# The first layer of a dense MLP by one level of Strassen's method, with the weights of both layers streamed

## The chip, the core and the metric

The kernel runs on one core of a Trainium2 chip. A core has TensorE (PE, matrix multiplication into PSUM), VectorE (DVE), ScalarE (ACT), GpSimd (POOL) and SyncE (SP, which only issues transfers here); sixteen DMA engines move data between device memory and SBUF. The metric is device time in microseconds for one launch.

## The reference, cut to what matters

Three stages follow one another: a decayed attention (8 batches, 8 heads, 576 tokens, 64 wide), a routed MLP (4608 tokens to 8 experts of 576 tokens each), and a dense MLP, which the change concerns:

```python
def _moe2_ref(x, w_in, w_out):       # x (4608, 512), w_in (512, 2048), w_out (2048, 512)
    h = x @ w_in
    relu6 = np.clip(h + 3.0, 0.0, 6.0)
    g = h * relu6 / 6.0
    return (g @ w_out).astype(np.float32)
```

The weights of the dense MLP are float64. The output is float32.

## The kernel before, in words

Every product is made of three matmuls, because TensorE multiplies a reduced form of float32 (`float32r`): an operand is split into a high half (rounded by ScalarE's copy) and a low half (VectorE: operand minus high half), and high x high, high x low and low x high are added up in PSUM. `mm3` issues the three.

The experts' stage. Expert r has two halves of 288 tokens and eight slices f of 128 hidden columns, 128 units in all. `A` makes a hidden slice (12 matmuls, 288 columns), ScalarE and VectorE split it, `Bm` multiplies it into four accumulators `y0` to `y3` (12 matmuls). `A` runs two units ahead of `Bm`. The experts' weights lie in six slots (`pairs`) of SBUF; the routing of the next experts, their weights' splitting and the gathering of their tokens run beside the matmuls.

The dense stage. The 4608 tokens are cut into NB = 12 blocks of 384, and the 2048 hidden columns into 16 slices f. `C` makes one hidden slice of one block (12 matmuls of 384 columns: 4 slices of the 512 inputs, 3 matmuls each), then ScalarE takes relu(h + 3), VectorE min(., 6) times h, ScalarE the high half, VectorE the low half. `Dm` multiplies it into three accumulators of 128 tokens x 512 (9 matmuls of 512 columns). `C` again runs two units ahead. All weights of both layers are in SBUF when the stage begins and stay there. At the end of a block three tiles `xg` take the accumulators, and GpSimd scatters their rows to the output. `yload` fetches the tokens of the next block (`yT`, what the experts' stage left) and splits them.

`convert` works beside the experts' stage: it turns the float64 weights (32 chunks of 128 x 512) into float32r halves with seven VectorE and three ScalarE instructions a chunk, and stores them in device memory (`w32`), except for the last two groups, which go straight into their slots. `w2load` brings the others into slots that the experts have left.

The order on each engine is fixed when the program is written: the main loop emits matmuls, and after each one `tick` counts down. A side job (`route`, `weights`, `xload`, `convert`, `yload`) is a generator; what it yields is the number of ticks, that is of matmuls, until its next instructions are emitted. So one tick is one matmul of the main loop, and the paces in `PARAMS` (`w_cv` and so on) are counted in them. Each engine then runs its own instructions in that order and waits on semaphores for the others.

Of the kernel before, what the change touches and what calls it, by code (L numbers as in the profile page):

```python
# [89 lines left out]
def _segs(**w):  # L90
    o, d = 0, {}
    for n, x in w.items():
# [8 lines left out]
NB, W2 = 12, 384  # L101
PARAMS = dict(w_first=30, w_cmp=11, w_hop=5, w_hop2=7, w_pe=2, w_low=5, w_pre=22, w_dec=16, w_add=1, w_t=2, w_load=40, w_load0=60, w_gran=16, w_half=8, w_gran0=24, w_gran1=10,
              w_xg=36, w_xg2=50, w_xt=40, w_xt0=4, w_cv=17, w_cv2=6, w_cv3=9, w_w2=60, n_nat=12)
GRAN = ((0, 0), (1, 0), (0, 1), (2, 0), (1, 1), (3, 0), (2, 1), (3, 1))
SLOT = (2, 3, 4, 5, 0, 1, 6, 7)
CONV, DIRECT = (2, 3, 4, 5, 6, 7, 0, 1), 2


class Kern:
# [14 lines left out]
    def later(self, n, do):  # L124
        self.due.append([n, do])
# [5 lines left out]
    def tick(self, n=1):  # L131
        for x in self.due:
            x[0] -= n
        while self.due and self.due[0][0] <= 0:
            self.due.pop(0)[1]()
        for name in list(self.side):
            s = self.side[name]
            s[1] -= n
            if s[1] <= 0:
                self.step(name)  # L140
# [491 lines left out]
    def convert(self):  # L632
# [4 lines left out]
        seq = [(g, w, hf) for g in CONV for w in range(2) for hf in range(2)]  # L637
        direct = 4 * (len(CONV) - DIRECT)

        def issue(i):  # L640
            g, w, hf = seq[i]
# [4 lines left out]
        def pace(late=False):  # L646
            return self.w_cv if "route" in self.side else self.w_cv3 if late else self.w_cv2
# [5 lines left out]
        for i, (g, w, hf) in enumerate(seq):  # L653
            raw, o = raws.pop(0), self.cvo[i % 2]
            if i >= direct:
                while self.pB < (self.w2_old[g] // 4) * 16 + 8 + 2 * (self.w2_old[g] % 4) + 2:
                    yield 1
                o = self.pairs[SLOT[g]][:, w, :, hf * n:hf * n + n]
            lo, hi = raw[:, :, 0], raw[:, :, 1]
            t0 = cv.tile([128, n], I32, name="c_t0")  # L660
# [13 lines left out]
            yield pace(True)  # L674
            V.scalar_tensor_tensor(o[:, 0], ta, 2.0 ** 30 - s0, t0.bitcast(F32), op0=OP.is_le, op1=OP.mult)
            nc.scalar.activation(ta, t1, AF.Copy, scale=2.0 ** -34)
            yield pace(True)
            V.tensor_scalar(t0, o[:, 0].bitcast(I32), -0x800000, None, op0=OP.bitwise_and)
            yield pace(True)
            V.tensor_tensor(o[:, 1], t0.bitcast(F32), ta, OP.mult)  # L680
            if i < direct:
                nc.sync.dma_start(self.w32[g, :, w, :, hf * n:hf * n + n], o.bitcast(F32))
            self.converted = i + 1
            yield pace(True)

    def w2load(self):
        for k, g in enumerate(CONV[:len(CONV) - DIRECT]):
            while self.converted < 4 * k + 4:
                yield 1
            while self.pA < 128 if g > 5 else self.pB < (self.w2_old[g] // 4) * 16 + 8 + 2 * (self.w2_old[g] % 4) + 2:  # L690
                yield 1
            self.nc.gpsimd.dma_start(self.pairs[SLOT[g]], self.w32[g])  # L692
            self.w2_ready = k + 1
            yield self.w_w2

    def need_w2(self, f, w):
        k, direct = CONV.index(f // 2), len(CONV) - DIRECT
        self.run_until("convert", lambda: self.converted >= (4 * k + 2 + 2 * w if k >= direct else 4 * k + 4))
        if k < direct:
            self.run_until("w2load", lambda: self.w2_ready > k)  # L700

    def yload(self):
        nc = self.nc
        for b in range(NB):
            while self.pB < 16 if b == 0 else (self.pD < (b - 1) * 16 or self.pC < b * 16 - (7 if b == 1 else 13)):
                yield 1
            d = self.yacts[b % 2]
            rs = {}

            def issue(k):  # L710
                rs[k] = self.r_p.tile([128, W2], F32, name="yr")
                nc.sync.dma_start(rs[k], self.yT[:, k, b * W2:b * W2 + W2])

            issue(0)
            issue(1)
            yield 40
            for k in range(4):
                x = rs.pop(k)
                nc.scalar.activation(d[0][:, k], x, AF.Copy)
                yield 10  # L720
                nc.vector.tensor_tensor(d[1][:, k], x, d[0][:, k].bitcast(F32), OP.subtract)
                if k + 2 < 4:
                    issue(k + 2)
                yield 20
# [7 lines left out]
    def mlps(self):  # L732
        nc, a = self.nc, self.a
        units = [(1, r, hb, f) for r in range(E) for hb in range(2) for f in range(8)]
        units += [(2, b, 0, f) for b in range(NB) for f in range(16)]
        hts, acc, scat = {}, {}, []
        banks = (("y0", "y1", "y2"), ("y3", "rt", "tp"))

        def A(u):
# [9 lines left out]
            h = self.hg_p.tile([128, 2, 288], FR, name="hg")  # L749
# [6 lines left out]
        def Bm(u):  # L756
# [7 lines left out]
            for d in range(4):  # L764
                c = (f % 2) * 512 + d * 128
                self.mm3(y[d], w[:, 0, c:c + 128], w[:, 1, c:c + 128], h[:, 0], h[:, 1], f == 0, f == 7)
            if f == 7:
                n0 = r * CAP + hb * 288
                last = (r, hb) == (E - 1, 1)
                for d in range(4):  # L770
                    if last and d < 2:
                        o = self.xg_p.tile([128, DM], F32, name="xg")
                    else:
                        o = self.r_p.tile([128, W2], F32, name="r" if d < 2 else "yr")
                    if last and d % 2:
                        nc.vector.tensor_copy(o[:, 0:288], y[d])
                    else:
                        nc.scalar.activation(o[:, 0:288], y[d], AF.Copy)  # L778
# [4 lines left out]
        def C(u):  # L783
            _, b, _, f = u
            self.run_until("yload", lambda: self.y_ready > b)
            if b == 0:
                self.need_w2(f, 0)
            w = self.pairs[SLOT[f // 2]][:, 0]
            y = self.yacts[b % 2]
            p = self.pp.tile([128, W2], F32, name="h", bufs=2)  # L790
            for k in range(NP):
                c = k * 256 + (f % 2) * 128
                self.mm3(p, w[:, 0, c:c + 128], w[:, 1, c:c + 128], y[0][:, k], y[1][:, k], k == 0, k == NP - 1)
            r = self.r_p.tile([128, W2], F32, name="r")
            nc.scalar.activation(r, p, AF.Relu, bias=self.bias[:, 0:1])  # L795
            nc.vector.scalar_tensor_tensor(r, r, 6.0, p, op0=OP.min, op1=OP.mult)  # L796
            g = self.hg_p.tile([128, 2, W2], FR, name="hg")
            nc.scalar.activation(g[:, 0], r, AF.Copy)  # L798
            nc.vector.tensor_tensor(g[:, 1], r, g[:, 0].bitcast(F32), OP.subtract)  # L799
            hts[u] = g  # L800
            self.pC += 1

        def Dm(u):
            _, b, _, f = u
            if b == 0:
                self.need_w2(f, 1)
            w = self.pairs[SLOT[f // 2]][:, 1]
            g = hts.pop(u)
            if f == 0:
                acc[b] = [self.pp.tile([128, 512], F32, name=n) for n in banks[b % 2]]  # L810
            c = (f % 2) * 512
            for t in range(3):
                x = slice(128 * t, 128 * t + 128)
# [153 lines left out]
```

## Time and profile before

| | us |
|---|---|
| median of three runs (lowest, highest) | 1494.48 (1492.3, 1495.27) |
| the profiled execution, its own time | 1491.7 |
| span in its profile, first to last instruction | 1489.3 |

The profiled execution's time is its span and 2.4 us around it; it is 2.8 us below the median of the runs. In rows of the profile, PE is a matmul and PEld the weight load that goes with each; L815 is a line of the kernel before. A matmul's own duration overlaps with the next one's, so the pace is read from the starts.

### The profile page before, as it was taken

The page shows a single profiled execution, that of the slowest core. Times are in us where ns is not written, and L with a number is a line of the kernel's source. Part 1 is how long each engine was busy: PE and PEld are TensorE (multiplying, and loading weights), DVE is VectorE, ACT ScalarE, POOL GpSimd, SP SyncE. Part 2 cuts the span into 40 slices and gives each one's busy share as a digit, 9 for nine tenths or more (in the row PEclk, how much of TensorE's full clock was granted, in tenths as well). Part 3 has the DMA queues.
Part 4 walks back from the last instruction along what each step waited for, and adds up shares of the span by engine and source line. Part 5 has one row for each costly group of instructions (what it writes and reads, how often), then busy time and mean ns, then how long its engine had stood idle before and what let it go on. Part 6 is the DMA issues. An engine that isn't in the chain of part 4 may idle for free.

```text
span 1489.3 us, 27253 instructions
## 1 busy us (share of the span) xinstructions
PE 1423.1 (96%) x11270; PEld 1301.3 (87%) x11270; DVE 702.8 (47%) x1729; ACT 529.9 (36%) x1031; POOL 233.3 (16%) x256
## 2 busy tenths in 40 slices
PE   7899588999999999999999999999999999999998
PEld 5777488989999999999999999999999999999997
DVE  3344557787788798773332323323232323323222
ACT  3233334453444445543332333323232333323222
POOL 6860213122132223000000000000000000000000
PEclk9999799999999999999999999999999999999999
DMA  9991625455464568648010100001010100000000
GB/s 377 378 318 63 234 61 179 160 183 162 134 207 135 176 199 265 190 144 320 22 43 7 37 22 22 32 11 43 1 43 7 37 22 22 32 12 32 1 22 22
DMA packets 60380, 162.90 MB, mean 109 GB/s; under 512 B 7520, under 2 KB 22112, under 8 KB 59488
## 3 DMA queue, kind: packets, MB, share of 16 engines
q1 hardware_dynamic: 41392, 92.10, 18.0%
q0 software_dynamic: 16032, 65.55, 13.3%
q10 hardware_dynamic: 2832, 3.52, 0.7%
q8 instruction: 88, 1.44, 0.4%
q14 instruction: 36, 0.29, 0.1%
HBM read 120.24 MB, written 40.89 MB: 108 GB/s over the span
## 4 chain that ended last, share of the span: by engine, by line
issue 51%; PE 3%; POOL 3%; POOLq 0%; ACT 0%
POOL out_dram L825 2%; PE y L729 2%; PE h L729 2%; POOL nop L831 0%; POOLq L963 0%; POOL big L692 0%; POOLq L825 0%; POOL pair L692 0%; ACT r L778 0%; ACT hg L750 0%; POOLq L692 0%
## 5 line engine op out<-in xcount | busy, mean ns | idle before, releaser
L796 DVE SCALAR_TENSOR_TENSOR r<-r,h 128x384 f32<-128x384 f32 x192 | 106.4, 554 | 445.1 <-ACT r L795 445.1
L729 PE MATMUL h<-big,pair 128*128 128x288 f32 (+1 forms) x1440 | 276.2, 311 | 0.5 <-ACT big L620 0.4
L795 ACT ACTIVATE r<-h,bias 128x384 f32<-128x384 f32 x192 | 111.5, 581 | 439.0 <-PE h L729 439.0
L729 PEld LDWEIGHTS h<-big,pair 128*128 128x128 f32 x1440 | 218.1, 189 | 5.0 <-issue 1.7
L729 PE MATMUL h<-big 128*128 128x288 f32 (+1 forms) x864 | 184.1, 317 | 0.4 <-DVE big L624 0.4
L729 PE MATMUL h<-yact,pair 128*128 128x384 f32 x768 | 173.3, 337 | 0.0
L729 PE MATMUL h<-yact,big 128*128 128x384 f32 x768 | 173.3, 336 | 0.0
L729 PE MATMUL y<-hg,pair 128*128 128x288 f32 x1056 | 167.0, 300 | 1.5 <-ACT r L778 1.5
L799 DVE TENSOR_TENSOR hg<-r,hg 128x384 fp32r<-128x384 f32 x192 | 107.3, 559 | 113.5 <-ACT hg L798 113.5
L825 POOL DMA_INDIRECT out_dram<-xg,idx x36 | 35.1, 975 | 761.4 <-ACT xg L824 754.9
L729 PEld LDWEIGHTS y<-hg,pair 128*128 128x128 f32 x1056 | 146.7, 188 | 3.0 <-ACT r L778 1.7
L815 PE MATMUL y<-pair,hg 128*128 128x512 f32 x576 | 148.9, 394 | 0.0
L815 PE MATMUL y<-big,hg 128*128 128x512 f32 x576 | 148.9, 394 | 0.0
L729 PEld LDWEIGHTS h<-yact,big 128*128 128x128 f32 x768 | 138.5, 188 | 6.4
L729 PEld LDWEIGHTS h<-yact,pair 128*128 128x128 f32 x768 | 138.3, 188 | 6.1
L798 ACT ACTIVATE hg<-r 128x384 fp32r<-128x384 f32 x192 | 100.7, 525 | 119.1 <-DVE r L796 119.1
L729 PEld LDWEIGHTS h<-big 128*128 128x128 f32 x864 | 137.3, 188 | 3.0 <-DVE big L624 0.6
L552 POOL DMA_INDIRECT raw<-in_w_dram,widx x64 | 68.5, 1070 | 361.7 <-issue 66.9
L815 PEld LDWEIGHTS y<-big,hg 128*128 128x128 f32 x576 | 106.7, 188 | 16.8
L815 PEld LDWEIGHTS y<-pair,hg 128*128 128x128 f32 x576 | 106.7, 188 | 16.6
L750 ACT ACTIVATE hg<-h 128x288 fp32r<-128x288 f32 x128 | 52.3, 408 | 120.6 <-PE h L729 112.9
L729 PE MATMUL y<-hg,big 128*128 128x288 f32 x480 | 78.5, 307 | 1.5 <-ACT r L778 1.5
(178 smaller groups left out, 1735.7 us busy)
## 6 DMA issues: line engine op xcount, KB each, us to landing
qk<-in_qk_dram SPq DMA_DIRECT2D x36, 512.0 KB
kv<-in_kv_dram SPq DMA_DIRECT2D x32, 512.0 KB
c_raw<-in_w_dram SPq DMA_DIRECT2D x32, 512.0 KB
w<-big SPq DMA_DIRECT2D x24, 512.0 KB
yr<-yT SPq DMA_DIRECT2D x48, 192.0 KB
big<-w POOLq DMA_DIRECT2D x4, 2048.0 KB
yT<-yr SPq DMA_DIRECT2D x32, 144.0 KB
yT<-r SPq DMA_DIRECT2D x30, 144.0 KB
```

Source lines behind the costliest of these rows:

```text
L552: nc.gpsimd.indirect_dma_start(out=raw, out_offset=None, in_=a[("w1", "w2")[w]], in_offset=bass.IndirectOffsetOnAxis(ap=self.widx[:, r, g: ...
L729: self.nc.tensor.matmul(out, w, x, start=(first and i == 0), stop=(last and i == 2))
L750: nc.scalar.activation(h[:, 0], p, AF.Relu)
L795: nc.scalar.activation(r, p, AF.Relu, bias=self.bias[:, 0:1])
L796: nc.vector.scalar_tensor_tensor(r, r, 6.0, p, op0=OP.min, op1=OP.mult)
L798: nc.scalar.activation(g[:, 0], r, AF.Copy)
L799: nc.vector.tensor_tensor(g[:, 1], r, g[:, 0].bitcast(F32), OP.subtract)
L815: nc.tensor.matmul(acc[b][t], g[:, gw, x], w[:, ww, c:c + 512], start=(f == 0 and i == 0), stop=(f == 15 and i == 2))
L825: ins = nc.gpsimd.indirect_dma_start(out=a["out"], out_offset=bass.IndirectOffsetOnAxis(ap=self.idx[:, 3 * b + t:3 * b + t + 1], axis=0), ...
```

## The change

The first layer of the dense stage takes blocks of 768 tokens (NB = 6) and two hidden slices at once, NS = 8 pairs of slices a block. In one such step, a span here (48 in all), its operands are 2 x 2 blocks: two halves of the 512 inputs, two halves of the 768 tokens, two hidden slices. Instead of eight products of blocks it makes seven of sums of blocks (Winograd's form): each is 6 matmuls of 384 columns. The sums of weights (`s1` to `s4`) are made in `convert`, those of tokens (`t1` to `t4`) in `yload`. The products are summed up partly in PSUM, by going on in a bank that has been read meanwhile, and partly on VectorE, through the tiles `m1`, `u2` and `tv`; `post` does what ScalarE and VectorE did in `C`. The second layer's 36 matmuls a span (`outs`) are those of the span before, and are issued between the products.

The converted weights no longer stay in SBUF. Those of the first layer (seven operands, 14 KB in each partition, 1835 KB a span) and of the second (8 KB, 1049 KB a span) are kept in device memory, `wC` and `wD`, and are fetched again for each span into two slots each, `cw` and `dw`, by `wload` and `dload` on GpSimd's queue.

```diff
-NB, W2 = 12, 384
+W2 = 384
+NB, NS = 6, 8
...
-              w_xg=36, w_xg2=50, w_xt=40, w_xt0=4, w_cv=17, w_cv2=6, w_cv3=9, w_w2=60, n_nat=12)
+              w_xg=36, w_xg2=50, w_xt=40, w_xt0=4, w_cv=14, w_cv2=9, w_cv3=7, w_y=10, w_y0=8, n_nat=12)
 GRAN = ((0, 0), (1, 0), (0, 1), (2, 0), (1, 1), (3, 0), (2, 1), (3, 1))
-SLOT = (2, 3, 4, 5, 0, 1, 6, 7)
-CONV, DIRECT = (2, 3, 4, 5, 6, 7, 0, 1), 2
+OPW, OPY = ("11", "s2", "12", "s3", "s1", "22", "s4"), ("11", "t2", "21", "t3", "t1", "t4", "22")
...
+        def store(o, q, op):
+            x = OPW.index(op) * 512
+            nc.sync.dma_start(self.wC[2 * q:2 * q + 2, :, x:x + 512].rearrange("f p x -> p f x"), two(o).bitcast(F32))
+
+        def split(x, q, op):
+            o = out()
+            h, l = two(o)[:, :, 0:256], two(o)[:, :, 256:512]
+            nc.scalar.activation(h, two(x), AF.Copy)
+            yield pace()
+            V.tensor_tensor(l, two(x), h.bitcast(F32), OP.subtract)
+            yield pace()
+            store(o, q, op)
...
+            if op == "22":
+                V.tensor_tensor(R2, R1, R2, OP.add)
+                yield pace()
+                yield from split(R2, q, "s1")
+            elif op == "11":
+                V.tensor_tensor(R1, x, R1, OP.subtract)
+                yield pace()
+                yield from split(R1, q, "s3")
+                V.tensor_tensor(R2, R2, x, OP.subtract)
+                yield pace()
+                yield from split(R2, q, "s2")
+            elif op == "12":
+                V.tensor_tensor(R2, x, R2, OP.subtract)
+                yield pace()
+                yield from split(R2, q, "s4")
+                self.dC = q + 1
...
+    def wload(self):
+        nc = self.nc
+        for s in range(NB * NS):
+            i = s % NS
+            while s == 0 and not self.freed(28) or s == 1 and not self.freed(29) or s > 1 and self.span < s - 1:
...
+            nc.gpsimd.dma_start(self.cw[s % 2], self.wC[i])
+            self.c_ready = s + 1
...
+    def dload(self):
+        for s in range(NB * NS):
+            i = s % NS
+            while not self.freed(30) or s > 1 and self.span < s:
...
+            self.nc.gpsimd.dma_start(self.dw[s % 2], self.wD[i])
+            self.d_ready = s + 1
...
+                yield from split(b11, "11")
+                t1 = b11
+                V.tensor_tensor(t1, b12, b11, OP.subtract)
+                yield w
+                V.tensor_tensor(b12, b22, b12, OP.subtract)
+                yield from split(t1, "t1")
+                V.tensor_tensor(t1, b22, t1, OP.subtract)
+                yield from split(b12, "t3")
+                yield from split(t1, "t2")
+                yield from split(b21, "21")
+                V.tensor_tensor(b21, b21, t1, OP.subtract)
+                yield from split(b22, "22")
+                yield from split(b21, "t4")
...
+            def prod(p, first):
+                o = n[0]
+                for kt in range(2):
+                    for j, (wh, yh) in enumerate(((0, 0), (0, 1), (1, 0))):
+                        nc.tensor.matmul(p, cw[:, o, wh, kt], y[o][:, yh, kt], start=(first and kt + j == 0),
+                                         stop=(kt == 1 and j == 2), skip_group_check=True)
+                        self.tick()
+                n[0] += 1
...
+            def post(x, key):
+                while open_r[0] > 1:
+                    self.due.pop(0)[1]()
+                open_r[0] += 1
+                r = self.r_p.tile([128, W2], F32, name="r")
+                nc.scalar.activation(r, x, AF.Relu, bias=self.bias[:, 0:1])
+
+                def two():
+                    V.scalar_tensor_tensor(r, r, 6.0, x, op0=OP.min, op1=OP.mult)
+
+                def three():
+                    gs[key] = g = self.gbuf[self.n_g % 5].rearrange("p (a b) -> p a b", a=2)
+                    self.n_g += 1
+                    nc.scalar.activation(g[:, 0], r, AF.Copy)
+
+                    def four():
+                        V.tensor_tensor(g[:, 1], r, g[:, 0].bitcast(F32), OP.subtract)
+                        low.add(key)
+                        open_r[0] -= 1
+
+                    self.later(4, four)
+
+                self.later(4, two)
+                self.later(8, three)
...
+            bank = lambda: self.pp.tile([128, W2], F32, name="h", bufs=2)
+            p = bank()
+            prod(p, True)
+            m1 = self.r_p.tile([128, W2], F32, name="yr")
+            nc.scalar.activation(m1, p, AF.Copy)
+            yield
+            p2 = bank()
+            prod(p2, True)
+            u2 = self.r_p.tile([128, W2], F32, name="yr")
+            V.tensor_tensor(u2, m1, p2, OP.add)
+            yield
+            prod(p, False)
+            post(p, (s, 0, 0))
+            yield
+            prod(p2, False)
+            V.tensor_tensor(tv, m1, p2, OP.add)
+            yield
+            p = bank()
+            prod(p, True)
+            V.tensor_tensor(tv, tv, p, OP.add)
+            post(tv, (s, 1, 1))
+            yield
+            prod(p2, False)
+            V.tensor_tensor(m1, m1, p2, OP.add)
+            post(m1, (s, 1, 0))
+            yield
+            prod(p, False)
+            V.tensor_tensor(u2, u2, p, OP.add)
+            post(u2, (s, 0, 1))
...
+            seq = [(0, t) for t in range(3)] + [(1, t) for t in range(3, 6)] + [(1, t) for t in range(3)] + [(0, t) for t in range(3, 6)]
...
+                for k, (gw, ww) in enumerate(((0, 0), (0, 1), (1, 0))):
+                    if k == 2:
+                        while (s, j, t // 3) not in low:
+                            self.due.pop(0)[1]()
+                    nc.tensor.matmul(acc[b][t], g[:, gw, x], w[:, 512 * ww:512 * ww + 512],
+                                     start=(i == 0 and seen[t] == 0 and k == 0), stop=(i == NS - 1 and seen[t] == 1 and k == 2))
+                    self.tick()
...
+        merge(prods(0), both(), (0, 1, 1) * 4)
+        for s in range(1, NB * NS):
+            merge(prods(s), outs(s - 1), (0, 1, 1) * 5 + (0, 1) * 2)
```

On TensorE in the middle of the dense stage of the kernel before, a group of 12 matmuls of the first layer (`h`, a new bank each time) alternates with 9 of the second (`y0` to `y2` are the accumulators, `yact`, `pair` and `big` hold tokens and weights):

```order
L729 MATMUL h_11487<-yact0_2221,big_2679 128x384 x12
L815 MATMUL y0_11378<-big_2679,hg_11442 128x512 x3
L815 MATMUL y1_11379<-big_2679,hg_11442 128x512 x3
L815 MATMUL y2_11380<-big_2679,hg_11442 128x512 x3
L729 MATMUL h_11517<-yact0_2221,big_2679 128x384 x12
```

In the changed kernel the beginning of a span stands there; `h_10558` and `h_10579` are its two banks, `ring`, `big` and `hgt` hold tokens, weights and hidden tiles:

```order
L876 MATMUL h_10558<-big_2679 128x384 x6
L970 MATMUL y0_10445<-ring_2221 128x512 x3
L970 MATMUL y1_10446<-ring_2221 128x512 x3
L876 MATMUL h_10579<-big_2679 128x384 x6
L970 MATMUL y2_10447<-ring_2221 128x512 x3
L970 MATMUL y3_10448<-ring_2221,hgt_2218 128x512 x3
L876 MATMUL h_10558<-big_2679 128x384 x6
L970 MATMUL rt_10449<-ring_2221,hgt_2218 128x512 x3
L970 MATMUL tp_10450<-ring_2221,hgt_2218 128x512 x3
L876 MATMUL h_10579<-big_2679 128x384 x6
L970 MATMUL y0_10445<-ring_2221,hgt_2218 128x512 x3
L970 MATMUL y1_10446<-ring_2221,hgt_2218 128x512 x3
```

The products came down to groups of 6, two of which (the third and fourth) go on in the banks of the first two, and one or two groups of the second layer, 3 matmuls each, stand between them; after these rows come the products 5 to 7 and five more groups of 3.

On VectorE in the dense stage of the kernel before, the work of three units and the splitting of a next block's tokens (`yact`):

```order
L721 TENSOR_TENSOR yact0_2221<-yr_9947,yact0_2221 128x384
L796 SCALAR_TENSOR_TENSOR r_10034<-r_10034,h_10018 128x384
L799 TENSOR_TENSOR hg_10037<-r_10034,hg_10037 128x384
L721 TENSOR_TENSOR yact0_2221<-yr_9992,yact0_2221 128x384
L796 SCALAR_TENSOR_TENSOR r_10064<-r_10064,h_10050 128x384
L799 TENSOR_TENSOR hg_10067<-r_10064,hg_10067 128x384
```

In the changed kernel these rows stand in the third span: `L915`, `L921` and `L925` are sums of products, `L889` and `L897` belong to `post`, `L788` splits tokens of the second block, and `L705`, `L714`, `L728` and `L672` are the converter's:

```order
L915 TENSOR_TENSOR yr<-yr,h 128x384
L788 TENSOR_TENSOR big<-yq,big 128x384
L705 TENSOR_TENSOR big<-c_t_9475,c_ta 128x2x256
L714 TENSOR_TENSOR c_ta<-big 128x512
L889 SCALAR_TENSOR_TENSOR r<-r,h 128x384
L728 TENSOR_TENSOR rec_2220<-c_ta,rec_2220 128x512
L897 TENSOR_TENSOR hgt<-r,hgt 128x384
L921 TENSOR_TENSOR L<-yr,h 128x384
L788 TENSOR_TENSOR big<-yq,big 128x384
L672 TENSOR_TENSOR big<-rec_2220,big 128x2x256
L925 TENSOR_TENSOR L<-L,h 128x384
L889 SCALAR_TENSOR_TENSOR r<-r,L 128x384
```

The converter and the splitting of tokens, which stood beside the experts' matmuls before, now reach into the first spans and stand between the sums and the hidden tiles.

On GpSimd's queue at the end of the experts' stage of the kernel before, the last converted weights come in and the scatters of the first block follow:

```order
L692 DMA big<-w_77 128x4096 x2
L692 DMA pair_2217<-w_77 128x4096
L692 DMA pair_2218<-w_77 128x4096
L692 DMA big<-w_77 128x4096 x2
L825 DMA out_dram<-xg,idx 4608x512
L831 MEMSET nop 128x1
```

In the changed kernel the first block's weights stand there (`wC` the first layer's, `wD` the second's):

```order
L747 DMA big<-wC 128x3584 x2
L757 DMA ring<-wD 128x2048 x2
L747 DMA big<-wC 128x3584 x2
L757 DMA ring<-wD 128x2048
L747 DMA big<-wC 128x3584
L757 DMA ring<-wD 128x2048
L747 DMA big<-wC 128x3584
L757 DMA ring<-wD 128x2048
L944 DMA out_dram<-xg,idx 4608x512
L950 MEMSET nop 128x1
```

The loads no longer end with the experts: a pair of them stands there for each span, and a block's six scatters stand between two pairs.

## Rows read from the trace of the kernel before

**Rows 1.** The page, parts 1 and 2: busy time, then 40 slices in tenths.
```profile
PE 1423.1 (96%) x11270; PEld 1301.3 (87%) x11270; DVE 702.8 (47%) x1729; ACT 529.9 (36%) x1031; POOL 233.3 (16%) x256
...
DVE  3344557787788798773332323323232323323222
...
DMA  9991625455464568648010100001010100000000
```

**Rows 2.** Windows: the experts, their end, the dense layer (columns: first row).
```profile
core 0: us, PE busy (x) PEld busy (x) DVE busy (x) ACT busy (x) POOL busy (x), PEclk, DMA share, GB/s
240.00:640.00 400.00, 382.09 (x3308) 368.28 (x3308) 316.14 (x905) 187.29 (x373) 93.01 (x88) 0.99 0.57 181
...
683.00:1482.00 799.00, 799.00 (x4006) 723.41 (x4004) 241.21 (x440) 240.33 (x450) 37.90 (x70) 1.00 0.09 31
```

**Rows 3.** Waits of TensorE from 240 to 640 us: total, times, longest.
```profile
engine line waited for: us in total, times, longest us
PE tp L614 <- DMA xg<-xn,idx: 3.9, 3, 2.2
PE y L729 <- ACT r L778: 2.9, 2, 1.5
PE rt L398 <- ACT gs L393: 2.7, 2, 1.5
```

**Rows 4.** Timeline of TensorE in the dense layer: start, length, count.
```profile
1000.56 2.27 PE L729 MATMUL h<-yact,big 128*128 128x384 f32 x12
1002.67 2.24 PE L815 MATMUL y<-big,hg 128*128 128x512 f32 x9
1004.75 2.27 PE L729 MATMUL h<-yact,big 128*128 128x384 f32 x12
```

**Rows 5.** The page, part 5: groups on VectorE and ScalarE, 384 wide.
```profile
L796 DVE SCALAR_TENSOR_TENSOR r<-r,h 128x384 f32<-128x384 f32 x192 | 106.4, 554 | 445.1 <-ACT r L795 445.1
...
L795 ACT ACTIVATE r<-h,bias 128x384 f32<-128x384 f32 x192 | 111.5, 581 | 439.0 <-PE h L729 439.0
...
L799 DVE TENSOR_TENSOR hg<-r,hg 128x384 fp32r<-128x384 f32 x192 | 107.3, 559 | 113.5 <-ACT hg L798 113.5
...
L798 ACT ACTIVATE hg<-r 128x384 fp32r<-128x384 f32 x192 | 100.7, 525 | 119.1 <-DVE r L796 119.1
```

**Rows 6.** Groups by line: the converter, and the low half of an expert's hidden tile.
```profile
L751 DVE SCALAR_TENSOR_TENSOR hg<-h,hg 128x288 fp32r<-128x288 f32 x128 | 58.1, 454 | 35.9 <-ACT hg L750 34.3 <-issue 0.8
...
L665 DVE SCALAR_TENSOR_TENSOR c_t<-c_raw,c_t 128x512 int32<-128x512 int32 x32 | 22.1, 690 | 0.4
...
L680 DVE TENSOR_TENSOR big<-c_t,c_ta 128x512 fp32r<-128x512 f32 x24 | 16.4, 685 | 0.6 <-ACT c_ta L676 0.6
...
L661 DVE TENSOR_SCALAR c_t<-c_raw 128x512 int32<-128x512 int32 x32 | 13.6, 426 | 0.2
```

**Rows 7.** Timeline of weight loads in an expert's layers, twelve to a row.
```profile
642.77 1.65 PEld L729 LDWEIGHTS h<-big,pair 128*128 128x128 f32 x12
644.37 1.65 PEld L729 LDWEIGHTS y<-hg,pair 128*128 128x128 f32 x12
```

**Rows 8.** Timeline of GpSimd: two weight loads of 2048 KB.
```profile
662.57 0.57 POOL L692 DMA_DIRECT2D big<-w  x1 [39.38 <-PE y L729]
668.96 0.55 POOL L692 DMA_DIRECT2D big<-w  x1 [5.83 <-PE y L729]
```

**Rows 9.** Window while those loads run; columns as in Rows 2.
```profile
669.00:676.00 7.00, 7.00 (x53) 7.00 (x52) 4.58 (x9) 2.72 (x5) 0.93 (x2) 1.00 1.01 415
```

**Rows 10.** Timeline of GpSimd: scatters of one block, and the last of the run.
```profile
750.04 1.03 POOL L825 DMA_INDIRECT out_dram<-xg,idx  x1 [65.41 <-ACT xg L824]
751.06 0.12 POOL L831 MEMSET nop<- 128x1 f32 x1
751.37 1.00 POOL L825 DMA_INDIRECT out_dram<-xg,idx  x1 [0.19 <-issue]
...
1484.19 0.97 POOL L825 DMA_INDIRECT out_dram<-xg,idx  x1 [0.19 <-issue]
```

More of the change, by code (lines that the diff above doesn't have):

```diff
@@ L124, in later @@
     def later(self, n, do):
-        self.due.append([n, do])
+        i = len(self.due)
+        while i and self.due[i - 1][0] > n:
+            i -= 1
+        self.due.insert(i, [n, do])
     def flush(self):
@@ L136, in tick @@
         for name in list(self.side):
+            if name not in self.side:
+                continue
             s = self.side[name]
@@ L644, in issue, with pace, out @@
             return raw
-        def pace(late=False):
-            return self.w_cv if "route" in self.side else self.w_cv3 if late else self.w_cv2
+        def pace():
+            return self.w_cv if "route" in self.side else self.w_cv2 if self.span < 0 else self.w_cv3
+        def out():
+            self.n_o += 1
+            return self.cvo[self.n_o % 2]
+        def store(o, q, op):
[9 more added lines that the diff above has]
+            store(o, q, op)
         while self.routed < 2:
@@ L704, in yload @@
         for b in range(NB):
-            while self.pB < 16 if b == 0 else (self.pD < (b - 1) * 16 or self.pC < b * 16 - (7 if b == 1 else 13)):
+            while b and self.span < max(1, NS * (b - 1)):
                 yield 1
[L707 to L715, printed above, removed]
@@ L716, in yload, with piece @@
-            yield 40
[L717 to L724, printed above, removed]
+            op = self.yops[b % 2]
+            w = self.w_y if b else self.w_y0
+            def piece(k, pool):
+                x = yq.tile([128, 2 * W2], F32, name="yq") if pool else self.raw_p.tile([128, 1024], F32, name="raw")[:, 0:2 * W2]
+                nc.sync.dma_start(x, self.yT[:, k, 2 * b * W2:2 * b * W2 + 2 * W2])
+                return x[:, 0:W2], x[:, W2:2 * W2]
@@ new lines, in evict @@
+        def evict(b, t):
+            o = self.xg_p.tile([128, DM], F32, name="xg")
+            if t % 2:
+                V.tensor_scalar(o, acc[b][t], 1.0 / 6.0, None, op0=OP.mult)
+            else:
+                nc.scalar.activation(o, acc[b][t], AF.Copy, scale=1.0 / 6.0)
+            ins = nc.gpsimd.indirect_dma_start(
+                out=a["out"], out_offset=bass.IndirectOffsetOnAxis(ap=self.idx[:, 6 * b + t:6 * b + t + 1], axis=0),
+                in_=o, in_offset=None)
+            for x in scat:
+                self.tc.declare_no_dep(ins.ins, x.ins, reason="each row of out is scattered to once")
+            scat.append(ins)
+            nc.gpsimd.memset(self.nop, 0.0)
@@ new lines, in merge, with both @@
+        def merge(x, y, pat):
+            for c in pat:
+                next((x, y)[c], None)
+            for _ in x:
+                pass
+            for _ in y:
+                pass
+        A(units[0])
+        A(units[1])
+        for i, u in enumerate(units[:-2]):
+            A(units[i + 2])
+            for _ in Bm(u):
+                pass
+        def both():
+            yield from Bm(units[-2])
+            yield from Bm(units[-1])
+        merge(prods(0), both(), (0, 1, 1) * 4)
```

241 lines of the change are left out of this document (120 added, 121 removed).

## The prediction, made before the changed kernel had run

> **What bounds the kernel now.** I read the page first. Matmuls cover 96% of the span [rows 1], and behind the attention the slices show two regimes: from slice 7 to 18 of 40 VectorE is at seven to nine tenths and the DMA engines at about half, and from there VectorE falls to two or three tenths and the DMA engines to nearly nothing. The windows say how tightly TensorE is bound in each. In the dense stage (683 to 1482 us) it is busy for all of 799.00 us [rows 2], so nothing but its own matmuls sets the pace there. In the 400 us of the experts before, it is idle for 17.9 us, with VectorE busy for 316 us of them [rows 2]; the waits are small and many, for routing, gathered tokens and emptied accumulators [rows 3]. So fewer matmuls in the dense stage shorten the run one to one, as long as the other engines and the transfers still fit beside them; and that stage has room: VectorE 30%, DMA 9% [rows 2].
>
> **What is removed.** Pace is read from starts. Twelve matmuls of 384 columns take 1000.56 to 1002.67, 2.11 us or 0.1758 us each; nine of 512 take 1002.67 to 1004.75, 2.08 us or 0.2311 us each [rows 4]. The work of a span was 48 + 36 matmuls, 4 x 4.19 = 16.76 us. It becomes 42 + 36: 7.38 + 8.32 = 15.70 us. Over 48 spans, 288 matmuls of 384 columns go: 288 x 0.1758 = **50.6 us**. The forms stay the same, and the last of 12 matmuls passes to the first of 9 without a gap [rows 4], so the many more changes between the two kinds are priced at nothing. The Trainium skill (TensorE: Matmul & The Clock Gate, Back-to-back issue gap) gives a warm matmul N / 2.4 ns + 2.5 ns; by it 384 columns would be an estimated 162.5 ns, and the gain 46.8 us. The row is 13 ns longer, and I keep the row.
>
> **VectorE in a normal span.** It gets 13 instructions of 384 columns: two for each of four hidden tiles (0.554 and 0.559 us [rows 5]) and five sums. A sum with one operand in PSUM does not occur before; its nearest row is the first of rows 5, which reads PSUM too, so 0.556. That is 7.2 us of 15.70. Each block's tokens add 22 such instructions, 12.2 us over about four and a half spans. ScalarE gets nine (0.525 to 0.581 us [rows 5]), 5 us. Both fit. I also followed the waits of TensorE inside a span, from the order: with a product P at 1.05 us and a group of the second layer O at 0.69, the third product goes on in the first bank 3.8 us after it was filled, and the copy in between takes 0.55. The tightest place is the sum after the sixth product: its bank is wanted by the next span's first product after O, P and O, 2.43 us, and the sum takes 0.56. So VectorE may lag by 1.9 us before TensorE notices. Cost: nothing, and this 1.9 us is the cover.
>
> **VectorE in the first spans.** Here the cover goes. The order puts the last converter instruction into the sixth span, and the second block's tokens are split from the second span on. From the second span's beginning to the converter's end there are 345 ticks: 4.4 spans, 69.4 us of TensorE. VectorE's rows in that stretch are 83 instructions of 384 columns (0.556 us), 30 of 512 (0.688, between the two rows of 0.685 and 0.690) and 16 of the short kind (0.426 [rows 6]): 46.1 + 20.6 + 6.8 = 73.5 us. It is over 100%: 4.1 us too much over the whole, and over its densest 263 ticks I count 6.9 us. Besides, where a hidden tile's second step stands right behind the sum it comes from (the last two rows of the order's VectorE piece), a late VectorE waits for ScalarE's relu of 0.58 us [rows 5] in between; two or three times a span that is up to 6.6 us more. Subtracting the 1.9 us of cover, the loss lies between 2 us (whole stretch, no such waits) and 16 (densest stretch, all the waits, and a lag of 2 to 3 us brought in from the stage before, where I count 37.8 us of VectorE in the 40.0 us of the last 300 expert matmuls at 1.60 us for twelve [rows 6, 7]). With half of the waits it is 5.5 by the whole stretch and 8.3 by the densest; I take **7 us**.
>
> **The converter beside the experts.** Its pace goes from 17 ticks to 14, and sums of weights are added. Between the same two ticks of the routing (303 and 2128) the order has 682 VectorE instructions in place of 671: 23 more of 512 columns at 0.685, and 12 fewer of the others (four each at 0.690, 0.426 and 0.556), 15.8 - 6.7 = 9.1 us more [rows 5, 6]. Its bounds are 0 (all of it falls into gaps) and 9 (all of it delays TensorE). In each of the seven routing rounds about 100 ticks already hold some 7 us more VectorE work than TensorE time, 49 us in all, and TensorE's idle time there is 17.9 [rows 2]; by that ratio, 0.36, it costs **3 us**. The larger number of stores on SP's queue (44 of 512 KB for 24) delays only the storing of expert results, whose buffers have the 25.6 us of the next eight units to come free.
>
> **The streams.** A span needs 1835 + 1049 KB. While loads of 2048 KB followed one another on the same queue, the engines moved 415 GB/s [rows 8, 9]; at that the pair takes 6.9 us. What one transfer costs beyond its bytes no row isolates; the last scatter, 256 KB, was issued at 1484.19 [rows 10] and the span ended at 1489.3, so 5.1 us less its 0.6 is an upper bound, 4.5. Both are issued when a span begins and wanted when the next begins: 11.4 of 15.70 us, so hidden. The first has no span ahead of it: its place in the order is 72 expert matmuls, 9.6 us [rows 7], ahead of the first product; 1835 KB take 4.4 + at most 4.5. Cost 0, at most 3 with the other transfers that run there.
>
> **Blocks' ends.** Six evictions share three `xg` tiles, so the fourth waits for the first's scatter. That begins about 9.9 us into the span, and one scatter is issued every 1.3 us [rows 10]; with the 5.1 us from above VectorE is held to 15.0, evicts, and makes the sixth product's sum by 16.3, where the bank is wanted at 15.7. That is 0 to 0.6 us at each of five block ends: **1 us** (0 to 3). GpSimd's next load stands behind these scatters, some 1 to 2 us late against 4.3 of slack. The end of the run keeps its form, three scatters after the last matmul.
>
> **The sum**, against the profiled execution's 1491.7: 1491.7 - 50.6 + 7 + 3 + 1 = **1452 us**. That execution lies 2.8 us below the median of the runs, which belongs to the range.
>
> **Rivals.** *All covered* (8%): VectorE's lag never passes the cover, and 1491.7 - 50.6 = 1441. For it speaks that routing rounds with 7 us too much cost only 2.6 each; against it, that here the excess is carried on over four spans. *VectorE binds hard* (10%): every upper bound at once, 1491.7 - 50.6 + 16 + 9 + 3 = 1469; it would show as VectorE at nine tenths and more over six spans. *The streams come late* (5%): the case on the other side. It needs loads that are slower beside this stage than [rows 9] shows. With the 11 us above spent, the gain of 1.055 us a span is used up when a span lasts 16.6 us; less 4.5, that is 2884 KB in 12.1 us, 238 GB/s. At 200 GB/s a span lasts 18.9 us and the run 1452 + 47 x 3.2 = 1602. The Trainium skill (SBUF — State Buffer, SBUF: two separate sides) has a mechanism for it: GpSimd, which writes the descriptors of its own queue's transfers, is shut out of a shared port while VectorE runs in a two-port mode. As a mechanism of this kernel: the converter's short instructions (0.426 us for 512 columns, [rows 6]) would be the ones, and two loads issued in the midst of them took 0.57 and 0.55 us on GpSimd [rows 8], so I see no such hold, and after the sixth span those instructions are gone.
>
> **Numbers.** The forecast has 77%. Its range by its own terms is 1443 to 1468 (losses between 2 and 27), which leaves out most of each rival. About 0.2%, 3 us, is what a measurement of this kernel can tell from no change; faster than that is 94%, the same 1%, slower 5%.
>
> **What would show it.** Right: 2016 first-layer matmuls at the same 0.176 us; a dense stage whose spans, from the seventh on, take 15.7 us with no idle TensorE; waits of TensorE for VectorE, some 7 us, in the second to sixth span alone; the experts' stage 3 us longer. Wrong: idle time before first products that DMA ends (the streams), spans above 15.8 us late in the run, or a wait for sums in every span, which would mean that the bank cover of 1.9 us is not what I read.

## The result, and the profile after

The changed kernel took 1453.95 us (median of 4 runs, 1450.24 to 1454.95) against 1494.13 for the kernel before: 0.9728 of its time, 95% interval 0.9708 to 0.9748. The prediction was 1452. The profiled execution took 1453.67 us, its span 1451.9; its page, parts 1, 2, 5 and 6, answers to [rows 1, 5]:

```profile
PE 1378.9 (95%) x10982; PEld 1254.1 (86%) x10982; DVE 892.2 (61%) x2105; ACT 572.2 (39%) x1127; POOL 281.3 (19%) x346
...
DVE  3334556777887888787795564465456446545443
...
PEclk9999789999999999999999999999999999999999
DMA  9992533454644556767867555565555545545551
...
L876 PE MATMUL h<-ring,big 128*128 128x384 f32 x1296 | 262.3, 337 | 2.9 <-DVE yr L929 2.7
...
L876 PE MATMUL h<-big 128*128 128x384 f32 x720 | 145.0, 336 | 0.0
...
big<-wC POOLq DMA_DIRECT2D x48, 1792.0 KB, 7.6
ring<-wD POOLq DMA_DIRECT2D x48, 1024.0 KB, 9.8
...
wC<-big SPq DMA_DIRECT2D x28, 512.0 KB, 3.0
```

The 2016 first-layer matmuls are there, with one wait to speak of before them. The DMA engines, nearly idle in the dense stage before, are now half busy to the end. Windows of the same run, with columns as in [rows 2], show a stretch of one span's length in which the converter still runs, and a long one behind it:

```profile
730.03:745.73 15.70, 15.70 (x79) 13.87 (x78) 15.00 (x31) 9.37 (x18) 0.99 (x3) 1.00 0.80 285
...
840.00:1400.00 560.00, 560.00 (x2786) 503.20 (x2785) 294.23 (x556) 200.57 (x384) 65.88 (x120) 1.00 0.56 206
```

In the second row TensorE has no idle time at all. Even in the first, with VectorE busy for 15.00 of 15.70 us, TensorE does not stop.

To place the rest I cut every run into three by its timeline of TensorE: up to the first expert product, from there to the first dense product, from there to the span's end. Taking 50.6 us from the dense stage before (814.4) leaves 763.8; the last column is what each run spent above that (for the eighth product, above 814.4).

| run | first expert product at | experts' stage | dense stage | above |
|---|---|---|---|---|
| before | 183.8 | 491.1 | 814.4 | |
| before, again | 189.2 | 494.8 | 814.5 | |
| after | 190.6 | 492.3 | 769.0 | 5.2 |
| after, again | 185.7 | 495.0 | 767.8 | 4.0 |
| converter held | 184.6 | 493.2 | 766.4 | 2.6 |
| converter held, again | 185.7 | 493.7 | 765.8 | 2.0 |
| second load later | 184.5 | 494.9 | 772.0 | 8.2 |
| last quarter not stored | 185.6 | 495.2 | 764.1 | 0.3 |
| converter faster beside experts | 184.7 | 505.7 | 766.9 | 3.1 |
| eighth product | 186.4 | 494.5 | 815.4 | 1.0 |
| first-layer loads doubled | 187.8 | 492.5 | 880.3 | 116.5 |

So the first profile lost 5.2 us in the dense stage, most of it at the first span's end: beside the run without the last quarter's stores its third span starts 4.2 us late (682.93 to 714.13 us, for 680.80 to 707.81 there), its sixth 5.0 us (the 0.8 us between are spread in pieces of TensorE's idle time too short to be listed as waits). Pieces of its timelines (SyncE's issues, VectorE, TensorE):

```profile
681.31 0.38 SPq L665 DMA_DIRECT2D wC<-big  x1
...
694.77 0.69 DVE L700 SCALAR_TENSOR_TENSOR big<-c_ta,c_t 128x512 fp32r<-128x512 f32 x1 [2.51 <-DMA wC<-big]
...
696.45 1.40 PE L876 MATMUL h<-ring,big 128*128 128x384 f32 x6 [2.71 <-DVE yr L929]
```

what the view of that one store (L665, 681 to 683 us) says of it:

```profile
who waited for it (us, times):
  DVE big L700: 2.5, 1
...
DMA to landing us min/median/max: 13.4/13.4/13.4
```

and windows of the same time:

```profile
690.00:695.00 5.00, 3.74 (x23) 3.42 (x21) 2.46 (x6) 1.66 (x4) 0.53 (x1) 1.00 1.07 378
695.00:700.00 5.00, 3.55 (x12) 3.07 (x13) 3.51 (x8) 2.49 (x6) 0.00 (x0) 0.76 1.02 373
700.00:705.00 5.00, 5.00 (x24) 4.47 (x24) 4.24 (x9) 2.10 (x5) 0.00 (x0) 0.90 0.99 348
...
698.00:699.00 1.00, 1.00 (x4) 0.73 (x3) 0.97 (x3) 0.05 (x1) 0.00 (x0) 0.50 1.02 416
...
701.00:702.00 1.00, 1.00 (x7) 0.95 (x6) 1.00 (x3) 0.00 (x0) 0.00 (x0) 1.00 0.95 374
```

The converter has two output tiles and fills them in turn. Its next chunk wants the tile whose last contents are still on their way to DRAM: the store issued at 681.31 lands 13.4 us later and lets VectorE go on at 694.77, where the median store took 3.0 us. (The store after it, issued at 687.32 from the other tile, took 8.7 us, and nobody waited for it.) The DMA engines are full, for the first loads of both layers run then. Behind the waiting instruction stands, in order, the sum that empties a bank (L929), and TensorE waits 2.71 us for it. Then its granted clock falls: the 0.76 and 0.90 of the two windows of 5 us are mixtures of the two levels, and windows of 1 us have it at 0.50 (1.2 GHz) from 698 to 701 us and at 1.00 again behind it. By these shares that cost an estimated 1.7 us more. VectorE is busy for only 2.46 of the 5 us from 690: it is held, not overloaded.

**Theory A**: the loss in the first spans is a converter store that lands late on full DMA engines. **Theory B**, the prediction's: it is VectorE's work.

### The profile page after: what moved, and what is told of

It reads as the page before. It is cut to its first block, busy times and chain, and to the rows that moved or that the text cites. A ratio compares the mean times of both kernels' runs of the same rounds, so it can differ in the third digit from the quotient of the medians.

```text
span 1451.9 us, 27422 instructions
## 1 busy us (share of the span) xinstructions
PE 1378.9 (95%) x10982; PEld 1254.1 (86%) x10982; DVE 892.2 (61%) x2105; ACT 572.2 (39%) x1127; POOL 281.3 (19%) x346
## 4 chain that ended last, share of the span: by engine, by line
PE 78%; DVE 11%; DMA 5%; issue 3%; ACT 2%; POOL 0%; POOLq 0%; ACTq 0%; DVEq 0%
PE h L876 22%; PE y L970 17%; PE h L808 10%; PE y L808 9%; PE rt L970 4%; PE tp L970 4%; DMA raw<-in_w_dram,widx 2%; PE ov L248 2%; PE sc L215 2%; DMA wC<-big 1%; DVE ring L576 1%; PE st L245 1%; PE y L327 1%; PE tp L619 1%; PE ov L238 1%
## 5 line engine op out<-in xcount | busy, mean ns | idle before, releaser
L876 PE MATMUL h<-ring,big 128*128 128x384 f32 x1296 | 262.3, 337 | 2.9 <-DVE yr L929 2.7
L876 PEld LDWEIGHTS h<-ring,big 128*128 128x128 f32 x1296 | 232.3, 188 | 23.6 <-DVE yr L929 4.0
L970 PE MATMUL y<-ring,hgt 128*128 128x512 f32 x684 | 180.2, 394 | 0.0
L808 PE MATMUL h<-big,ring 128*128 128x288 f32 x1056 | 171.6, 304 | 1.3 <-DVE hgt L829 0.8
L808 PE MATMUL y<-hgt,ring 128*128 128x288 f32 x1056 | 167.0, 300 | 0.0
L808 PEld LDWEIGHTS h<-big,ring 128*128 128x128 f32 x1056 | 149.4, 191 | 3.9 <-issue 1.7
L808 PEld LDWEIGHTS y<-hgt,ring 128*128 128x128 f32 x1056 | 146.9, 188 | 2.4 <-issue 2.4
L876 PE MATMUL h<-big 128*128 128x384 f32 x720 | 145.0, 336 | 0.0
L970 PEld LDWEIGHTS y<-ring,hgt 128*128 128x128 f32 x684 | 126.7, 188 | 19.9
L897 DVE TENSOR_TENSOR hgt<-r,hgt 128x384 fp32r<-128x384 f32 x114 | 63.5, 557 | 41.6 <-ACT hgt L894 40.4
L889 DVE SCALAR_TENSOR_TENSOR r<-r,h 128x384 f32<-128x384 f32 x48 | 26.6, 554 | 94.4 <-ACT r L886 94.3
L886 ACT ACTIVATE r<-h,bias 128x384 f32<-128x384 f32 x48 | 27.9, 580 | 125.6 <-PE h L876 125.6
```

Source lines behind the costliest of these rows:

```text
L808: self.nc.tensor.matmul(out, w, x, start=(first and i == 0), stop=(last and i == 2))
L876: nc.tensor.matmul(p, cw[:, o, wh, kt], y[o][:, yh, kt], start=(first and kt + j == 0), stop=(kt == 1 and j == 2), skip_group_check=True)
L886: nc.scalar.activation(r, x, AF.Relu, bias=self.bias[:, 0:1])
L897: V.tensor_tensor(g[:, 1], r, g[:, 0].bitcast(F32), OP.subtract)
L970: nc.tensor.matmul(acc[b][t], g[:, gw, x], w[:, 512 * ww:512 * ww + 512], start=(i == 0 and seen[t] == 0 and k == 0), stop=(i == NS - 1 an ...
```

## The experiments

**Both kernels again.** The first profile after also starts its experts 6.8 us later than the one before.

> The changed kernel once more, for a second profile of it. In its first profile the first expert product starts 6.8 us later than in the profile of the kernel before (190.6 against 183.8), with a granted clock of 0.57 and 0.75 in 150 to 170, in a stretch whose instructions are the same in both kernels. If that is a difference between executions, the new profile has the product within some 3 us of 183.8, or at another time than 190.6; if it belongs to the kernel, at 190.6 again. The 5 us lost at the end of the first span of the dense stage (VectorE held 2.5 us by the store of a converted chunk, TensorE waiting 2.7 us, then a granted clock of 0.5) should come back by theory A and by theory B alike. Time by all: 1451 to 1455.

> The kernel before once more, for a second profile of it: whether its first expert product starts at 183.8 again and its granted clock in 150 to 170 is 1.00 again. If the 6.8 us ahead of the experts are a difference between executions, these move by some us here too; if they belong to the changed kernel, they stay within 1 us.

The changed kernel took 1450.23 us in the second series: 0.9723 of before (0.9702 to 0.9745). The kernel before was run once more for its profile, 1500.2 us. Windows of the two new profiles, before first, then after:

```profile
150.00:160.00 10.00, 8.84 (x71) 8.30 (x70) 3.10 (x9) 4.79 (x9) 0.00 (x0) 0.52 0.48 183
160.00:170.00 10.00, 7.67 (x105) 6.74 (x102) 4.99 (x18) 5.34 (x11) 0.00 (x0) 0.97 0.69 264
```

```profile
150.00:160.00 10.00, 7.93 (x99) 7.01 (x98) 4.28 (x15) 5.93 (x12) 0.00 (x0) 0.91 0.65 240
160.00:170.00 10.00, 6.66 (x94) 5.99 (x94) 4.99 (x21) 4.95 (x10) 0.00 (x0) 1.00 0.81 298
```

Now the kernel before is the one at half clock (0.52), with its first expert product at 189.2, and the changed one is at 185.7. Over nine profiles of the kernels with the change in the table that point lies between 184.5 and 190.6: it differs between executions, and the 6.8 us are no effect of the change. In the new profile of after the dense loss is 4.0 us, in waits of 1.04, 0.81 and 1.02 us spread over two spans, the granted clock staying at 1.00; VectorE and ScalarE again wait for `wC<-big` ahead of the first two (0.84 and 3.38 us).

**The converter held back in the first span.**

```diff
+            while self.pB >= 124 and self.span < 1:
+                yield 1
             raw, o = raws.pop(0), out()
```

> The converter begins no chunk during the first span of the dense stage; its work there moves into the spans behind it. Theory A: the 5 us are lost because the converter's store lands late while the first loads of the dense stage fill the DMA engines, so that VectorE, in order, waits 2.5 us for a converter tile and TensorE for VectorE; without chunks there nothing waits, and the time falls by about 4.5 us (2.7 us of wait and 1.8 us at half clock) to 1449. Theory B, the prediction's: VectorE has too much work in the first spans; then more of it in spans 1 to 5 costs as much there, and the time stays at 1454 or rises by up to 3 us.

1447.2 us, 0.9693 (0.9676 to 0.9711), beside 1450.23 on the same chip; their runs do not overlap (1445.93 to 1448.24, 1449.53 to 1454.62). A second series gave 1448.85, 0.9690 (0.9669 to 0.9712). B's "same or slower" falls. (Of the 4.3 us between the two profiled executions only 1.4 lie in the dense stage; the rest lies ahead of it, in the first two columns of the table, where executions differ anyway.) A's 4.5 us were too many: of 4.0, 2.0 to 2.6 stay, for the wait came back, smaller, in the third span (L702 and L931 are L700 and L929 of the changed kernel; VectorE's timeline, then TensorE's):

```profile
717.28 0.69 DVE L702 SCALAR_TENSOR_TENSOR big<-c_ta,c_t 128x512 fp32r<-128x512 f32 x1 [1.86 <-DMA wC<-big]
...
721.74 1.31 PE L878 MATMUL h<-ring,big 128*128 128x384 f32 x6 [1.24 <-DVE yr L931]
```

**The second load of second-layer weights a span later.**

```diff
-            while not self.freed(30) or s > 1 and self.span < s:
+            while not self.freed(30) or s > 0 and self.span < s:
```

> The second load of second-layer weights (1 MB) is issued one span later, so that the stretch in which the DMA engines are full carries 1 MB less; VectorE's work is untouched. Theory A: at the 385 GB/s of that stretch 1 MB takes 2.7 us, the store of the converted chunk lands that much sooner, the wait of 2.7 us goes or shrinks and the half clock behind it with it: 2 to 4.5 us faster, 1449.5 to 1452. Theory B (too much VectorE work): no change.

1453.23 us, 0.9731 (0.9713 to 0.9750): neither theory's number, and some 3 us more than after on the same chip, though the runs of the two overlap (1451.84 to 1454.34, 1449.53 to 1454.62). The dense stage of its profile lost 8.2 us, for 4.0. The timelines of SyncE, ScalarE and TensorE show why:

```profile
695.41 13.41 SPq L665 DMA_DIRECT2D wC<-big  x3
...
707.08 0.63 ACT L670 ACTIVATE big<-rec 128x512 fp32r<-128x512 f32 x1 [6.26 <-DMA wC<-big]
...
708.95 1.32 PE L876 MATMUL h<-ring,big 128*128 128x384 f32 x6 [3.66 <-DVE L L925]
```

and the windows:

```profile
700.00:705.00 5.00, 5.00 (x26) 4.34 (x24) 1.93 (x4) 0.81 (x2) 0.00 (x0) 1.00 1.05 386
705.00:710.00 5.00, 1.34 (x8) 1.05 (x7) 1.52 (x3) 1.64 (x3) 0.00 (x0) 1.00 0.33 126
710.00:715.00 5.00, 4.45 (x14) 3.45 (x13) 4.83 (x11) 3.21 (x7) 1.08 (x2) 0.53 0.80 264
```

The megabyte left one full stretch for another (share 1.05 at 700 to 705), in which the converter has three stores to make. ScalarE waits 6.26 us for the tile of the store issued at 695.41, VectorE for ScalarE, TensorE for VectorE, and the clock halves behind it. My expectation looked at the store that had been late, not at the next ones. The mechanism is A's.

**All arithmetic, the last quarter's stores left out.**

```diff
             x = OPW.index(op) * 512
+            if q == 3:
+                return
...
-            nc.gpsimd.dma_start(self.cw[s % 2], self.wC[i])
+            nc.gpsimd.dma_start(self.cw[s % 2], self.wC[i if i < 6 else i - 2])
```

(the same for `wD`.)

> The converter does all of its arithmetic, but does not store the operands of the last quarter of the weights; spans 6 and 7 of each block load those of spans 4 and 5 instead (part of the output is computed with the wrong weights, with as much work). Theory A, as it stands after the three kernels before: what costs some 4 us in the first three spans is a converter store that lands late on full DMA engines, with ScalarE or VectorE waiting for its tile; without these stores that wait is gone and the time falls to that of the kernel that holds its converter back or below, 1445 to 1447.5. Theory B: it is VectorE's own work there (14.5 to 15 of 15.7 us in spans 2 to 4); that is unchanged, and so is the time, 1450.

1446.39 us, 0.9671 (0.9648 to 0.9694). All waits of TensorE from 683 to 1440 us:

```profile
PE h L879 <- DVE yr L932: 0.3, 1, 0.3
```

and two windows with the converter at work:

```profile
712.20:727.90 15.70, 15.70 (x79) 14.10 (x78) 14.50 (x30) 8.92 (x18) 1.06 (x2) 1.00 0.59 219
...
743.60:759.30 15.70, 15.70 (x79) 14.10 (x78) 15.18 (x32) 9.88 (x20) 1.07 (x2) 1.00 0.42 148
```

VectorE does the same work, 14.50 and 15.18 us of 15.70, and TensorE never waits there: 0.3 us of loss is left of 4 to 5, and the interval of the ratio lies clear of that of after (0.9702 to 0.9745). This decides for A. What it can't tell apart is the store's own lateness and the room that its bytes take from others; the waits above name the store.

**The converter faster beside the experts.**

```diff
...
-w_cv=14, w_cv2=9,
+w_cv=14, w_cv2=6,
...
```

> The converter's pace in the experts' stage goes from 9 to 6, so that it ends as the dense stage begins and neither its VectorE work nor its stores fall into the first spans. Both theories: the 4 us of the first spans are won back. What differs is the experts' stage: by the prediction's term for the converter beside the experts (7 instructions of 0.6 us more per 35 us cost 3 us there) a third more of converter work in the experts' stage costs 3 us or more again, and the time is 1449 to 1453; if that term is nothing, as the first profile has it, the time is 1445 to 1447.

1461.09 us, 0.9774 (0.9748 to 0.9799): slower than either number. The experts' stage grew from 493.9 (mean of the other eight runs with the change above) to 505.7. From 590 to 690 us, first after (second profile), then this run:

```profile
590.00:690.00 100.00, 100.00 (x744) 100.00 (x743) 78.17 (x152) 52.31 (x105) 9.86 (x11) 1.00 0.71 241
```

```profile
590.00:690.00 100.00, 94.58 (x688) 92.79 (x687) 88.47 (x174) 56.13 (x108) 9.77 (x10) 0.98 0.75 257
```

VectorE goes from 78 to 88 us of 100 and TensorE loses 5.4, half of it waiting for VectorE, half for ScalarE (2.7 us each). The first window takes in 9.3 us of the dense stage; up to 680 us, where both kernels are among the experts, VectorE has 71.6 and 80.0 us of 90, and TensorE loses the same 5.4. Where the rest of the 11.8 us lies was not followed up. A dense span bears 15 of 15.7 us, this stage does not bear 88%. Somewhere between the paces 9 and 6 the converter begins to cost.

In the dense stage 3.1 us are lost all the same, for the converter did not end ahead of it: its last three stores are issued between 687 and 702 us. TensorE's longest wait there is for ScalarE, where the copy that it needs stands behind a converter instruction whose input is late (ScalarE, TensorE):

```profile
695.16 0.77 ACT L688 ACTIVATE c_ta<-c_raw,bias 128x512 f32<-128x512 int32 x1 [2.58 <-DMA c_raw<-in_w_dram]
...
697.11 1.31 PE L876 MATMUL h<-ring,big 128*128 128x384 f32 x6 [1.56 <-ACT yr L910]
```

So a load that lands late on full DMA engines (share 1.03 and 1.05 from 690 to 700 us) does here what a late store did above.

**An eighth product.**

```diff
+            for kt in range(2):
+                for wh, yh in ((0, 0), (0, 1), (1, 0)):
+                    nc.tensor.matmul(p, cw[:, 6, wh, kt], y[6][:, yh, kt], start=False, stop=(kt == 1 and wh == 1),
...
```

> An eighth product of six matmuls in every span of the dense stage (product 7 is added a second time, so the output changes), with no other work. If the span is set by TensorE alone at 0.176 us a matmul, as the prediction has it, 288 matmuls of 384 columns cost 50.6 us again: 1450 + 50.6 = 1501, less what now covers the waits of the first spans (up to 4 us): 1497 to 1501. If other engines or the streams set the span of 15.7 us, a good part of it is free: under 1490.

1499.73 us, 1.0037 (1.0018 to 1.0055). Against the run without late stores the dense stage is 815.4 - 764.1 = 51.3 us longer. Of that 1.3 are waits in the first spans (1.6 us for `yr`, L929, where that run has 0.3), which leaves 50.0 for the predicted 50.6. In the middle of the stage one span's load follows the other's after 16.73 us (issues at 1012.59 and 1029.32), in the changed kernel after 15.69 (1028.42 and 1044.11). TensorE alone sets the span.

**First-layer loads doubled.**

```diff
+            for _ in range(1 if s < 8 else 2):
-            nc.gpsimd.dma_start(self.cw[s % 2], self.wC[i])
+                nc.gpsimd.dma_start(self.cw[s % 2], self.wC[i])
```

> From the ninth span on the first-layer operands are loaded twice into the same tile: 4.7 MB in a span instead of 2.9. By the rates of the first profile (372 to 388 GB/s when the DMA engines are full) 4.7 MB take 12.5 us of a span of 15.7. If the streams have the room that the prediction gives them (11.4 of 15.7 us landed), the second load still lands in time and the time stays at 1450 to 1451; if the room is smaller, each of 40 spans waits up to some us: 1490 and above.

1561.79 us, 1.0446 (1.0416 to 1.0477): a dense stage 112.5 us longer than in the second profile of after, 2.8 us for each of 40 spans in the mean. I had divided bytes by the rate of full engines. Issues of GpSimd:

```profile
1016.72 0.53 POOL L748 DMA_DIRECT2D big<-wC  x1 [9.76 <-PE h L877]
1024.81 0.53 POOL L748 DMA_DIRECT2D big<-wC  x1 [7.57 <-DMA big<-wC]
1025.33 0.54 POOL L758 DMA_DIRECT2D ring<-wD  x1
```

The second load waits until the first has landed, 8.1 us, the second layer's load stands behind both, and the first can't begin before TensorE has left the tile: a chain, not a sum of bytes (the engines moved 283 GB/s from 1000 to 1110 us). Of the 70 us that TensorE waits behind 770 us, 31.4 are for the two loads and 27.1 for VectorE's sum (L930), in five waits eight spans apart, at the blocks' ends. For the kernel itself it says that the pair has some microseconds to spare in a span, and not a second load's 8.

**The held kernel, with the second layer's load issued earlier.**

```diff
-            while not self.freed(30) or s > 1 and self.span < s:
+            while not self.freed(30) or s > 1 and self.span < s - 1:
                 yield 1
+            if s > 1:
+                yield 60
```

> The kernel that holds its converter back in the first span, with one thing more: from the third span on the second-layer load is issued about 4 us before its span begins, and no longer in the same microsecond as the first-layer load, so that the two bursts of 1 and 1.8 MB follow each other. Theory A (stores that land late on full DMA engines): what is left of the loss there, 2.6 us in the first dense spans of the held kernel, shrinks, and the time is 1 to 2 us under that of the held kernel. Rival: POOL, in order, waits for the second-layer tile to come free and issues the next first-layer load late; then single spans wait for it and the time rises by 1 to 10 us. If neither, the held kernel's time.

1781.61 us, 1.1913 (1.1882 to 1.1944), and not for the rival's reason. In the program the load now stands ahead of the last second-layer matmuls that read the same tile; these take the next span's weights (so part of the output is computed with wrong ones) and wait for them. Waits of TensorE behind 690 us:

```profile
PE rt L974 <- DMA ring<-wD: 231.5, 46, 9.9
```

The second layer reads its tile until after the next span has begun. Whether loads that are spread out would remove the last 2 us stays open. A third output tile for the converter, which by theory A would be the direct cure, was not tried.

## Why the prediction held, and which step did not

- *What is removed* (50.6): right. The steady span is 15.69 us, and an eighth product costs 50.0 us. The Trainium skill's formula (TensorE: Matmul & The Clock Gate, Back-to-back issue gap), which that section gives for an isolated matmul, made it 46.8, which the trace does not bear out.
- *VectorE in a normal span* (0): right; 294 of 560 us, no idle TensorE.
- *VectorE in the first spans* (7): this step failed in its reason; that its size held, 4.0 and 5.2 us, was luck. I found VectorE at 73.5 us of work in 69.4; from 701.6 to 771.0 the profile has it busy for 60.9. I had read TensorE's pace from starts, and VectorE's from lengths. Four rows of VectorE's timeline after show what that does:

```profile
736.20 0.55 DVE L915 TENSOR_TENSOR yr<-yr,h 128x384 f32<-128x384 f32 x1
736.67 0.68 DVE L705 TENSOR_TENSOR big<-c_t,c_ta 128x512 fp32r<-128x512 f32 x1
737.27 0.55 DVE L788 TENSOR_TENSOR ring<-yq,ring 128x384 fp32r<-128x384 f32 x1
737.74 0.42 DVE L686 TENSOR_SCALAR c_t<-c_raw 128x512 int32<-128x512 int32 x1
```

  They start 0.47, 0.60 and 0.47 us apart, each 0.08 us less than its length, since the end of one lies over the beginning of the next. The Trainium skill says so (Perfetto Trace Analysis, Optimizing Scalar/DVE Operations): the write-acknowledgement part of a profiled length overlaps with the next instruction. Here the trace agrees, at 0.08 us. If all 129 instructions start 0.08 us early (an estimate from these three gaps), that is 10.3 us: 63.2 of 69.4, under the bound. (The profile has 122 instructions in its stretch.) What cost the time was the converter's late store, which I had put down under the experts as harmless and had not followed into the stretch of the first loads. Even the place was off: the ends of the first and second span before all, not the second to sixth.
- *The converter beside the experts* (3): mis-sized, by little. 493.9 us against 492.9 (mean of the two before) is some 1 us, less than the 2.9 us between the least and the most of the eight, so it can't be told from nothing. The mechanism is real: a pace of 6 costs 11.8.
- *The streams* (0): right. The pair has landed 9.8 us after its issue, where I allowed 11.4. The doubled loads, at 1562, are what the rival of late streams (1602) looks like.
- *Blocks' ends* (1): nothing; no wait of TensorE behind 780 us.

The sum missed by 2 us in each series, too low in the first and too high in the second, and that is luck in part. From profile to profile the first series reads 1489.3 - 50.6 + 5.2 (dense stage) + 1.2 (experts' stage) + 6.8 (start of the experts) = 1451.9 us, the span of the profile after. The three small terms, 11 us in the sum, came to 6.4, each of them smaller than I had put it, and the 6.8 us, which are no effect of the change, made up for it.

## What to carry to other kernels

Add up an engine's work by the distance of starts in a run of instructions that follow closely, never by the lengths of rows: by the estimate above the difference turned 91% into 106% here. When a change fills the DMA engines in a stretch, list every transfer in it whose landing frees or fills a buffer, stores too; an in-order engine that waits for such a buffer holds all that stands behind it, and moving a load away can move the collision to the next store. Holding the converter back for one span, two lines, gave the fastest kernel here that leaves no work out: 1447.2 and 1448.85 us in two series.

## What the runs showed that I had not expected

A wait of TensorE of 2.71 us, and one of 3.66, were followed by half clock for some microseconds (0.50 from 698 to 701 us; 0.53 in a 5 us window), while waits of 0.7 to 1.6 us left it at 1.00. From 150 to 160 us, ahead of the experts, the eleven profiles have granted clocks from 0.52 to 1.00 for the same instructions: the three at 0.52 to 0.57 have the latest starts of the experts, 187.8 to 190.6 us, the others, at 0.91 to 1.00, lie between 183.8 and 186.4. That is more than most terms of this prediction. And a store of 512 KB took from 3.0 us (median) to 13.4 with the DMA engines full.
